# Two projection slots between the middle units of a four-unit cycle of an attention loop

## The chip, the cores and the metric

The kernel runs on one core of a Trainium2 chip. The metric is the device time of one execution in microseconds. A core has TensorE (PE in the profile; PEld are its weight loads), VectorE (DVE), ScalarE (ACT), GpSimd (POOL), SyncE (SP, which issues the DMAs here), a working memory SBUF and the accumulators PSUM, into which TensorE writes and from which VectorE and ScalarE read.

## The reference

One block of 2048 tokens of width 512, in float32. Two branches are mixed by a gate per token:

```python
g = sigmoid((x * gate_w).sum(-1, keepdims=True))
out = g * attention(x) + (1 - g) * glu(x)

# attention: 32 heads of 16, causal, window of 256 keys
qkv = x @ wqkv                                # 512 -> 3 * 512
scores = einsum("bhqd,bhkd->bhqk", q, k) * 16 ** -0.5
mask = (i - j >= 0) & (i - j < 256)
p = softmax(where(mask, scores, -1e9))
a = einsum("bhqk,bhkd->bhqd", p, v) @ wo

# gated linear unit, inner width 1376
b = (sigmoid(x @ w_gate) * (x @ w_up)) @ w_down
```

## The kernel before, in words

To keep float32 accuracy on a faster matmul type, most operands are split into a high part (a ScalarE cast) and a low part (a VectorE subtraction, raw minus high), and a product is made of three: high by high, high by low, low by high.

The program has three stages. First x and the weights are split, the values and the first query and key projections are made. Then comes the attention loop over 128 *units*: 8 groups of 4 heads, each with 16 blocks of 128 queries. Last, from 558 us on, come the down projection of the gated linear unit and the output projection. The change is in the loop.

A unit u has four *heads* h = 0 to 3, and each head emits, in the order of the code:

- s(u,h), `s_part`: the scores of one query block against up to three key blocks, one matmul of 64 contraction rows and up to 384 columns into a PSUM tile `s`. There are two such buffers. VectorE then adds the mask and takes the row maximum in one pass (L331, here *the reduction*; a short accumulator read follows). s(u,h) can't begin until the reduction of two heads before has left its buffer.
- st(u-9, h^1), `st_part`: nine units later, when the row maxima have come back by way of DRAM into spare contraction rows, the scores are computed again, transposed, into a PSUM tile `st` of three buffers; ScalarE takes the exponential (L380).
- one entry of a list of pending VectorE operations (`behind`) and one of pending ScalarE operations (`acts`).
- `run_slots(n)`: n *slots*. This is *gap* (u mod 4, h).

A slot is one step of the projections: work that does not depend on the attention of the unit. It holds two matmuls of 512 columns: one on contraction rows 0 to 63 for one group, one on rows 64 to 127 for a group that began 19 steps earlier (`SHIFT`). TensorE runs the two halves of its rows side by side; s and st of a head also take one half each. A group is one projected tile (`pj`, queries and keys; `gu`, gate and up) and takes 12 steps in each half; every 12 slots one group ends. At its end ScalarE copies it out of PSUM (L522 for `gu`, L270 for `pj`); three PSUM buffers (`misc`) are shared by the groups. A `pj` is then cast (L280, `sh`) and its low half subtracted (L284, `sl`), each one head later, through `acts` and `behind`. `gu` weights are split the same way (L506, L507), once per four groups, and the weights of a `pj` group of heads once per 16 units (L155, L157).

Every four units a *burst* multiplies the exponentials with the values (L428, `pvs` and `pvst`, in one `s` and one `st` buffer). It stands ahead of head 0 of units with u mod 4 = 2. ScalarE copies one half of it out (L442) and VectorE adds the other (L445). Behind the burst two slots run at once, and the gaps (2,0) and (2,1) have one slot less (`head`).

So a cycle of four units has had these slots, heads 0 to 3: u mod 4 = 0: 3, 3, 3, 3; 1: 3, 3, 3, 0; burst and 2; 2: 2, 2, 3, 3; 3: 3, 3, 3, 0. They are 42. At gap (1,3) the burst follows; at gap (3,3), between units 4k+3 and 4k+4, s(u,3) is followed by s(u+1,0) with nothing between but st. At the end of a unit 4k+3 three small VectorE operations (L343, L344, L347) are put into `behind` for the heads that follow.

The order is written out by hand: each engine runs its instructions in the order in which the code emits them, and semaphores hold them where an operand or a buffer is not ready.

Of the kernel before, what the change touches and what calls it, by code (L numbers as in the profile page):

```python
# [20 lines left out]
HG = 4  # L21
# [23 lines left out]
LAG = 9  # L45
# [3 lines left out]
HOLD = 2  # L49
GAP = 3  # L50
SHIFT = 19
WD_LATE = {0: 9, 2: 10}
WD_SPLIT = {0: 7, 1: 8, 3: 9, 5: 10}
AHEAD = 5
# [3 lines left out]
def gated_mix_kernel(  # L58
# [49 lines left out]
    NU = NG * NB  # L108
# [3 lines left out]
    def load_d(f):  # L112
        tag = "draw" if f in (6, 7) else "wqraw"
        raw_d[f] = cpool.tile([P, D], F32, tag=tag, name=f"wdraw{f}", bufs=2)
        nc.sync.dma_start(raw_d[f][0:FCH[f]], wd[f * P:f * P + FCH[f], :])
# [13 lines left out]
    with ExitStack() as actx:  # L129
# [14 lines left out]
        def load_wqk(g):  # L144
            raw = cpool.tile([P, ND, P], F32, tag="wqraw", name=f"wqraw{g}", bufs=2)
            nc.sync.dma_start(raw, wqk[g])
            return raw
# [138 lines left out]
        def stack_build(t):  # L286
            sh, sl = (v.bitcast(F32) for v in stg.pop(t))
            rt = ring[t % RING].bitcast(F32)
            st = rt.rearrange("(a r) j f -> r a j f", r=4)
            dmas = [fill_rows(t % RING, 0, 0)]  # L290
            for low in range(2):
                for j in range(4):
                    for r in range(3):
                        if low == (r == (1 if j < 2 else 2)):
                            dmas.append((st[r + 1, :, j], (sl if low else sh)[32 * j:32 * j + 32]))
            return dmas

        def run_dmas(dmas):
            for dst, src in dmas:
                nc.sync.dma_start(dst, src)  # L300
# [55 lines left out]
        def max_load(s):  # L356
            st = ring[s // 2 % RING].bitcast(F32).rearrange("(a r) j f -> r a j f", r=QB)
            o = s % 2 * CH
            nc.sync.dma_start(
                st[0, :, 0:2, o:o + CH], max_d[s].rearrange("(p s) l b t -> (s l) p (b t)", p=2),  # L360
            )
# [37 lines left out]
        def v_load(g):  # L399
            nc.sync.dma_start(  # L400
                vg[g % 2][:, 0:NB * GW].rearrange("p (b w) -> p b w", w=GW),
                v_d[:, :, g * GW:(g + 1) * GW].rearrange("b p w -> p b w"),
            )
# [90 lines left out]
        def load_gu(f, w):  # L494
            raw_gu[f, w] = cpool.tile([P, D], F32, tag="draw", name=f"guraw{f}_{w}", bufs=2)
            src = wgu[f, w] if FCH[f] == P else wgu_tail[w, :, :, 0:width(f, w)]
            nc.sync.dma_start(gu_half(raw_gu[f, w], width(f, w)), src)
# [63 lines left out]
        def turns():  # L561
            k3 = 3 * ND
            groups = []
            for t in range(n_rest * k3 + SHIFT):
                if t % k3 == 0 and len(groups) < n_rest:
                    groups.append((work or rest).pop(0))
                for half, v in enumerate((t, t - SHIFT)):
                    if 0 <= v < n_rest * k3:
                        groups[v // k3][0](v % k3, half)
                if t >= SHIFT and (t - SHIFT) % k3 == k3 - 1:  # L570
                    _, after, post = groups[(t - SHIFT) // k3]
                    post()
# [8 lines left out]
        def wo_load(t):  # L581
            raw = cpool.tile([P, CH2], F32, tag="hb", name=f"woraw{t}", bufs=4).rearrange("p (d n) -> p d n", d=2)
            nc.sync.dma_start(raw, wo_v[:, 2 * t:2 * t + 2])
            wo_raw.extend(raw[:, d] for d in range(2))

        def wo_split(d):
            nc.scalar.copy(wo_h[d], wo_raw[d])
            behind.append(lambda: nc.vector.tensor_tensor(
                wo_l[d], wo_raw[d], wo_h[d].bitcast(F32), op=ALU.subtract))

        def flush(acts):
            while acts:
                acts.pop(0)()
# [36 lines left out]
        def run_slots(n):  # L630
            for _ in range(n):
                next(slots, None)
# [22 lines left out]
        for u in range(N):  # L655
            if u == LAG + 2:
                vctx.close()
                ppool = actx.enter_context(tc.tile_pool(name="ppool", bufs=1))
                for k in range(2):
                    vg.append(ppool.tile([P, NB * GW + 16], F32, name=f"vg{k}"))  # L660
                    nc.gpsimd.memset(vg[k][:, NB * GW:], 0.0)
                hvs += [
                    v.rearrange("p (w t) -> p w t", t=CH)
                    for v in [vg[0][:, 0:2 * CH]] + [region[:, o:o + 2 * CH] for o in HVO]
                ]
            if u == LAG + 3 or u % NB == 0 and 0 < u < NU:
                v_load(u // NB)
            if u == 4:
                load_gu(0, 0)
                load_gu(0, 1)  # L670
            if (u % 8 == 1 and u > 16 or u == LAG + 1) and u // 8 + 1 < NP:
                sdma = stack_build(u // 8 + 1)
            if u % 16 == 8 and u // 16 + 2 < NG:
                raw_q = load_wqk(u // 16 + 2)
            if u % 4 == 1 and 1 < u <= NU + 1:
                max_load(u // 4 - 1)
            run_dmas(later)
            later.clear()
            run_dmas(sdma[:SD])
            del sdma[:SD]  # L680
            if u in (WO, WO + 2):
                wo_load((u - WO) // 2)
            if u == N - 4:
                acts.extend(lambda d=d: wo_split(d) for d in range(ND))
            if WD <= u < WD + 18 and (u - WD) % 2 == 0:
                load_d((u - WD) // 2)
            s4 = {U_LAST: NSTEP - 2, U_LAST + 1: NSTEP - 1}.get(u)
            if u % 4 == 3 and u > 11 and (u + 2) // 4 + 4 < NSTEP - 2:
                s4 = (u + 2) // 4 + 4
            if s4 is not None:  # L690
                work.append(proj_group(s4))
            if u >= NU + PVLAG - HOLD and rest:
                hold_group(*rest.pop(0))
            for hh in range(HG):
                if hh == 0 and u % 2 == 0:
                    if u in bursts:
                        pv_burst(*bursts[u])
                if hh == 0:
                    head = min(2, bursts.get(u, (0, 0))[1] // 2)
                    run_slots(head)  # L700
                if u < NU:
                    s_part(u, hh)
                if 0 <= u - LAG < NU:
                    st_part(u - LAG, hh ^ 1 if u < NU else hh)
                if u < LAG:
                    flush(behind)
                    run_slots(GAP)
                    flush(acts)
                    flush(behind)
                else:  # L710
                    if behind:
                        behind.pop(0)()
                    if acts:
                        acts.pop(0)()
                if hh == 2 and u % 4 == 0 and 0 < u <= NU:
                    max_store(u // 4 - 1)
                if u >= LAG and (hh < HG - 1 or u % 2 == 0 or u >= NU):
                    run_slots(GAP - (hh < head))
            if u % 4 == 3 and u < NU:
                behind[0:0] = max_split(u // 4)  # L720
            if u // 16 + 2 < NG:
                if u % 16 == 13:
                    acts.append(lambda g=u // 16 + 2, r=raw_q: (
                        split_wqk(g, r, 0), behind.append(lambda: split_wqk(g, r, 1))))
            if 0 <= u - LAG < NU:
                mask_p(u - LAG)
            if WD + 2 <= u < WD + 16 and (u - WD) % 2 == 0:
                acts.append(lambda f=(u - WD) // 2 - 1: split_d(f, True))
            if SUMS <= u and (u - SUMS) % 4 == 0:
                sums_load((u - SUMS) // 4)  # L730
            if SUMS + 2 <= u and (u - SUMS) % 4 == 2:
                behind.append(lambda c=(u - SUMS) // 4: later.append(sums_invert(c)))
            if u >= HLOAD and (u - HLOAD) % 2 == 0:
                h_load((u - HLOAD) // 2)
            if u >= N - 2:
                flush(acts)
                flush(behind)
            if u >= N - 4:
                run_dmas(later)
                later.clear()  # L740
                if u < N - 1:
                    h_skew(u - N + 1)
# [43 lines left out]
        for n, (c, f) in enumerate(steps):  # L786
# [3 lines left out]
            h_skew(n)  # L790
            if n in WD_LATE:
                load_d(WD_LATE[n])
            if n in WD_SPLIT:
# [87 lines left out]
```

## Time and profile before

| | |
|---|---|
| median of 3 runs | 738.99 us (738.47 to 740.3) |
| profiled execution, own time | 738.34 us |
| its span (first to last instruction) | 736.6 us |
| granted TensorE clock | 1.00 throughout |

Busy time of the engines by stretch of the span, in us:

| stretch | PE | PEld | DVE | ACT |
|---|---|---|---|---|
| 50 to 80 | 29.50 | 27.31 | 22.88 | 10.43 |
| 80 to 505 (loop) | 424.98 | 347.20 | 289.98 | 285.68 |
| 505 to 560 | 55.00 | 45.38 | 24.11 | 39.32 |
| 560 to 736.6 | 172.89 | 139.99 | 106.10 | 77.27 |

How to read the lines: a group's line names the source line, engine, operation, the tiles out<-in, partitions and elements, the count, then busy time and mean ns of one, then the idle time of the engine just before it and what ended most of that. A waits line says who waited for whom: us in total, times, longest. A timeline line has start in us, duration in us, engine, source line, operation, tiles, count, and in brackets the idle time before it with its releaser. Matmuls are pipelined: the next one of a half starts while the last still drains, so the pace of TensorE is read from start to start, and its busy share is not a measure of its pace.

### The profile page before, as it was taken

The numbers are of one execution on the slowest core, as the hardware profiler recorded it, in microseconds if no ns is written. First come the engines' busy times: TensorE is split into PE (matmuls) and PEld (weight loads), VectorE is DVE, ScalarE is ACT, GpSimd is POOL, SyncE is SP. The second block draws the span as 40 slices with busy tenths as digits, with TensorE's granted clock in tenths as the row PEclk, the third lists the DMA queues.
The fourth block names the chain that finished last, engine by engine and source line by source line (L and its number), as shares of the span: only waits on it lengthen the run. The fifth ranks groups of instructions, "written<-read, shape, count | busy, mean of one in ns | idle before, by whom it ended". The sixth has DMA issues, their size and how long they took to land.

```text
span 736.6 us, 20433 instructions
## 1 busy us (share of the span) xinstructions
PE 730.0 (99%) x7772; PEld 599.0 (81%) x7772; DVE 463.2 (63%) x1425; ACT 434.2 (59%) x898; POOL 165.9 (23%) x256
## 2 busy tenths in 40 slices
PE   8999999999999999999999999999999999999997
PEld 7889888888878878888887878888887888888886
DVE  4437767766676666765677667666424777557471
ACT  5512776676676667666667666666676554535241
POOL 7000433233233223233223322332330000000000
PEclk9999999999999999999999999999999999999999
DMA  8473564455455355444545525653555868466441
GB/s 296 114 231 113 131 174 137 110 134 152 126 136 134 108 150 147 137 120 121 156 125 137 135 57 160 181 168 108 169 174 164 244 206 257 149 214 202 148 135 57
DMA packets 88753, 112.68 MB, mean 153 GB/s; under 512 B 36050, under 2 KB 45778, under 8 KB 88656
## 3 DMA queue, kind: packets, MB, share of 16 engines
q1 hardware_dynamic: 88656, 111.39, 51.7%
q8 instruction: 61, 1.00, 0.6%
q14 instruction: 36, 0.29, 0.1%
HBM read 49.72 MB, written 36.45 MB: 117 GB/s over the span
## 4 chain that ended last, share of the span: by engine, by line
PE 98%; DMA 1%; DVE 0%; ACT 0%; issue 0%; SPq 0%; DVEq 0%
PE gu L258 37%; PE pj L258 10%; PE pvs L428 8%; PE s L325 7%; PE pd L80 6%; PE pd L82 5%; PE pd L81 5%; PE st L375 5%; PE vps L240 3%; PE pa L80 2%; PE pa L82 2%; PE pa L81 2%; PE pvst L428 2%; PE vps L80 1%; PE vps L81 1%; PE vps L82 1%
## 5 line engine op out<-in xcount | busy, mean ns | idle before, releaser
L331 DVE CUSTOM_DVE_ANT_0 junk<-s,mask 128x384 f32<-128x384 f32 (+2 forms) x512 | 266.5, 530 | 153.8 <-PE st L375 89.4
L258 PE MATMUL gu<-xh,w 64*128 64x512 f32 (+2 forms) x1392 | 352.5, 394 | 0.0
L380 ACT ACTIVATE region<-st 128x384 f32<-128x384 f32 (+2 forms) x512 | 239.2, 475 | 101.4 <-PE st L375 54.1
L258 PE MATMUL gu<-xl,w 64*128 64x512 f32 (+2 forms) x696 | 243.8, 394 | 0.0
L258 PEld LDWEIGHTS gu<-xh,w 64*128 64x128 f32 (+2 forms) x1392 | 204.9, 182 | 16.0 <-issue 0.8
L385 POOL TENSOR_SCALAR_AFFINE_SELECT region<-region 128x512 f32<-128x512 f32 x128 | 84.6, 661 | 378.3 <-ACT region L380 336.4
L375 PE MATMUL st<-ring 64*128 64x384 f32 (+2 forms) x536 | 168.5, 326 | 0.0
L325 PE MATMUL s<-ring 64*128 64x384 f32 (+2 forms) x536 | 167.1, 326 | 0.5 <-DVE mx L331 0.5
L258 PEld LDWEIGHTS gu<-xl,w 64*128 64x128 f32 (+2 forms) x696 | 124.9, 183 | 10.0 <-issue 2.0
L325 PEld LDWEIGHTS s<-ring 64*128 64x128 f32 x536 | 98.1, 184 | 28.7 <-DVE mx L331 18.5
L375 PEld LDWEIGHTS st<-ring 64*128 64x128 f32 x536 | 97.5, 184 | 6.9 <-ACT region L380 0.2
L258 PE MATMUL pj<-xh,wqh 64*128 64x512 f32 (+1 forms) x240 | 94.5, 399 | 0.0
L258 PE MATMUL pj<-xl,wqh 64*128 64x512 f32 (+1 forms) x240 | 93.0, 393 | 0.0
L428 PE MATMUL pvs<-region,vg 64*32 64x320 f32 (+4 forms) x1440 | 74.5, 346 | 0.0
L258 PE MATMUL pj<-xh,wql 64*128 64x512 f32 (+1 forms) x240 | 74.3, 396 | 0.0
L428 PE MATMUL pvst<-region,vg 64*32 64x320 f32 (+4 forms) x1440 | 73.1, 341 | 0.0
L390 POOL TENSOR_SCALAR_AFFINE_SELECT region<-region 128x512 f32<-128x512 f32 x112 | 72.0, 643 | 0.0
L428 PEld LDWEIGHTS pvs<-region,vg 64*32 64x32 f32 x1440 | 49.0, 106 | 26.8 <-issue 9.8
L80 PE MATMUL pd<-ring,hb 128*128 128x512 f32 (+1 forms) x176 | 69.4, 394 | 0.0
L82 PE MATMUL pd<-ring,hb 128*128 128x512 f32 (+1 forms) x176 | 68.9, 392 | 0.0
L81 PE MATMUL pd<-ring,hb 128*128 128x512 f32 (+1 forms) x176 | 68.6, 390 | 0.0
L76 ACT CAST hb<-region 128x512 fp32r<-128x512 f32 (+1 forms) x37 | 23.0, 622 | 51.5 <-DVE region L614 36.4
(83 smaller groups left out, 1040.1 us busy)
## 6 DMA issues: line engine op xcount, KB each, us to landing
gu_scratch<-sp SPq DMA_DIRECT2D x80, 256.0 KB
region<-gu_scratch SPq DMA_DIRECT2D x68, 256.0 KB
ring<-sh SPq DMA_DIRECT2D x128, 128.0 KB
ring<-sl SPq DMA_DIRECT2D x64, 128.0 KB
guraw<-in_wgu_dram SPq DMA_DIRECT2D x20, 256.0 KB
v_scratch<-region SPq DMA_DIRECT2D x16, 272.0 KB
vg<-v_scratch SPq DMA_DIRECT2D x8, 544.0 KB
region<-in_xT_dram SPq DMA_DIRECT2D x16, 256.0 KB
```

Of the source, the lines that this page charges most:

```text
L76: nc.scalar.copy(hi, src)
L80: mm(ps, lh, rh, start=first, stop=False)
L81: mm(ps, lh, rl, start=False, stop=False)
L82: mm(ps, ll, rh, start=False, stop=last)
L258: mm(pt[0:fw], (wl if w == 2 else wh)[r, d], (xl if w == 1 else xh)[r, d, c * CH:(c + 1) * CH], start=k == 0 and half != 1, stop=k == 3 * ...
L325: mm(pt[:, (k - k0) * P:(e - k0) * P], lhsT, blk(g, k, hh, 1, e - k), start=k == k0, stop=e == i + 1, skip_group_check=True,)
L331: nc.vector.tensor_tensor_reduce(junk[:, 0:n], pt[:, 0:n], mask[:, 3 * P - n:], scale=1.0, scalar=NEG, op0=ALU.add, op1=ALU.max, accum_out ...
L375: mm(pt[:, (q - j) * P:(e - j) * P], lhsT, blk(g, q, hh, 0, e - q), start=q == j, stop=e == last, skip_group_check=True,)
L380: nc.scalar.activation(pts[u][:, hh, 0:n], pt[:, 0:n], AF.Exp, scale=SCALE)
L385: nc.gpsimd.affine_select(p[:, :, 0:P], p[:, :, 0:P], pattern=[[0, HG], [1, P]], compare_op=ALU.is_ge, fill=0.0, base=0, channel_multiplie ...
L390: nc.gpsimd.affine_select(p[:, :, 2 * P:], p[:, :, 2 * P:], pattern=[[0, HG], [-1, P]], compare_op=ALU.is_gt, fill=0.0, base=0, channel_mu ...
L428: mm(acc[half][32 * hh:32 * hh + 32, q0:q1], vg[g % 2][r, c:c + 32], pts[g * NB + j][r, hh, q0 + o:q1 + o], start=m == 0, stop=m == len(or ...
```

## The change

The number of slots of a gap comes from a table by u mod 4 and head, from unit 12 on; before that, and behind the last unit of scores, nothing changes. Gap (3,3) gets 2 slots where it had none; gaps (1,1) and (3,1) have 2 where they had 3. The sum of a cycle stays 42. (1,3), ahead of the burst, stays 0.

```diff
+GAPS = ((3, 3, 3, 3), (3, 2, 3, 0), (3, 3, 3, 3), (3, 2, 3, 2))
...
-                if u >= LAG and (hh < HG - 1 or u % 2 == 0 or u >= NU):
-                    run_slots(GAP - (hh < head))
+                if u >= LAG:
+                    run_slots((GAP if u >= NU else GAPS[u % 4][hh] if u > LAG + 2 else GAP * (u % 2 == 0 or hh < HG - 1)) - (hh < head))
```

No instruction is added or removed; some change places. The new table is one line, so the lines of the changed kernel behind it have numbers higher by one. Three places follow, with the names in full: s67_3 is s of unit 67, head 3; the last number of a name only counts tiles.

TensorE, from s(67,3) to the first slots of unit 68 (gap (3,3)), before:

```order
L325 MATMUL s67_3_5135<-ring_63 128x384
L375 MATMUL st58_2_5139<-ring_63 128x384
L325 MATMUL s68_0_5150<-ring_63 128x384
L375 MATMUL st59_1_5154<-ring_63 128x384
L258 MATMUL pj21_5115<-xh_70,wqh5_4733 128x512
```

and now:

```order
L326 MATMUL s67_3_5131<-ring_63 128x384
L376 MATMUL st58_2_5135<-ring_63 128x384
L259 MATMUL pj21_5115<-xh_70,wqh5_4731 128x512
L259 MATMUL gu4_2_0_4925<-xh_70,w0_72 128x512
L259 MATMUL pj21_5115<-xl_71,wqh5_4731 128x512
L259 MATMUL gu4_2_0_4925<-xh_70,w0_72 128x512
L326 MATMUL s68_0_5150<-ring_63 128x384
```

Two slots, four matmuls, now stand between the two s.

TensorE, gap (1,1) of unit 69, before:

```order
L325 MATMUL s69_1_5232<-ring_63 128x384
L375 MATMUL st60_0_5236<-ring_63 128x384
L258 MATMUL gu4_0_1_5192<-xh_70,w0_72 128x512
L258 MATMUL pj21_5115<-xh_70,wqh5_4733 128x512
L258 MATMUL gu4_0_1_5192<-xh_70,w0_72 128x512
L258 MATMUL pj21_5115<-xl_71,wqh5_4733 128x512
L258 MATMUL gu4_0_1_5192<-xh_70,w0_72 128x512
L258 MATMUL pj21_5115<-xh_70,wqh5_4733 128x512
L325 MATMUL s69_2_5246<-ring_63 128x384
```

and now:

```order
L326 MATMUL s69_1_5232<-ring_63 128x384
L376 MATMUL st60_0_5236<-ring_63 128x384
L259 MATMUL gu4_0_1_5192<-xh_70,w0_72 128x512
L259 MATMUL pj21_5115<-xh_70,wqh5_4731 128x512
L259 MATMUL gu4_0_1_5192<-xh_70,w0_72 128x512
L259 MATMUL pj21_5115<-xl_71,wqh5_4731 128x512
L326 MATMUL s69_2_5244<-ring_63 128x384
```

The third slot of the gap has gone to the gap behind it, and everything up to gap (3,1) stands one slot later against s and st, from there to gap (3,3) two.

VectorE, unit 70, where a projection ends one slot later against the heads and its low half (sl) follows, before:

```order
L331 ISA junk70_2_5355,mx17_5149<-s70_2_5353,mask_155 128x384
L331 ISA mx17_5149 128x1
L284 TENSOR_TENSOR sl20_5099<-pr21_5339,sh20_5098 128x512
L331 ISA junk70_3_5369,mx17_5149<-s70_3_5367,mask_155 128x384
L331 ISA mx17_5149 128x1
```

and now:

```order
L332 ISA junk70_2_5352,mx17_5149<-s70_2_5350,mask_155 128x384
L332 ISA mx17_5149 128x1
L332 ISA junk70_3_5366,mx17_5149<-s70_3_5364,mask_155 128x384
L332 ISA mx17_5149 128x1
L285 TENSOR_TENSOR sl20_5097<-pr21_5346,sh20_5096 128x512
```

The subtraction stands behind the reduction of head 3 instead of that of head 2. So it is with every odd projection from 9 to 29 (units 22, 30, ... 102); the even ones, 8 to 28 (units 19, 27, ... 99), keep their place between the reductions of heads 1 and 2 of unit 4k+3.

## The prediction

> **What bounds the kernel now.** I read the busy shares and the groups of the page first, then the waits, then the timeline around the place that is changed.
>
> ```profile
> PE 730.0 (99%) x7772; PEld 599.0 (81%) x7772; DVE 463.2 (63%) x1425; ACT 434.2 (59%) x898; POOL 165.9 (23%) x256
> ...
> L331 DVE CUSTOM_DVE_ANT_0 junk<-s,mask 128x384 f32<-128x384 f32 (+2 forms) x512 | 266.5, 530 | 153.8 <-PE st L375 89.4
> L325 PE MATMUL s<-ring 64*128 64x384 f32 (+2 forms) x536 | 167.1, 326 | 0.5 <-DVE mx L331 0.5
> L325 PEld LDWEIGHTS s<-ring 64*128 64x128 f32 x536 | 98.1, 184 | 28.7 <-DVE mx L331 18.5
> ...
> PEld s L325 <- DVE mx L331: 18.5, 71, 0.9
> PEld st L375 <- ACT region L380: 0.2, 1, 0.2
> ```
>
> TensorE sets the end. Its matmul rows hardly show a wait (0.5 us ahead of s), because a matmul that is still draining counts as busy. The weight loads do show it: 71 of the loads of s stood 18.5 us for VectorE, those of st 0.2 us for ScalarE. So the one wait of the loop is that of s for one of its two PSUM buffers, which the reduction of two heads before (L331) has to leave.
>
> The page "Perfetto Trace Analysis" of the Trainium skill, section "Identifying the Most-Contended Engine", says that matmul busy time is no good measure of the distance to the roofline, and that the busy share of the weight loads serves better. The two L325 rows agree: by the first this change could win at most 0.5 us, by the second up to some 18.5 us stand ahead of the s loads.
>
> How much of such a wait costs time is read at unit 67 to 68, the old direct succession from gap (3,3).
>
> ```profile
> 294.10 0.34 PE L325 MATMUL s<-ring 64*128 64x384 f32 x1
> 294.27 0.39 PE L258 MATMUL pj<-xl,wqh 64*128 64x512 f32 x1
> 294.51 0.39 PE L258 MATMUL pj<-xh,wqh 64*128 64x512 f32 x1
> ...
> 294.95 0.33 PE L325 MATMUL s<-ring 64*128 64x384 f32 x1
> 295.29 0.44 PE L325 MATMUL s<-ring 64*128 64x384 f32 x1
> 295.57 0.39 PE L258 MATMUL pj<-xh,wqh 64*128 64x512 f32 x1
> ...
> 294.73 0.18 PEld L325 LDWEIGHTS s<-ring 64*128 64x128 f32 x1
> 295.29 0.18 PEld L325 LDWEIGHTS s<-ring 64*128 64x128 f32 x1 [0.36 <-DVE mx L331]
> ...
> 294.07 0.69 DVE L284 TENSOR_TENSOR sl<-pr,sh 128x512 fp32r<-128x512 f32 x1
> 294.67 0.55 DVE L331 CUSTOM_DVE_ANT_0 junk<-s,mask 128x384 f32<-128x384 f32 x1
> ```
>
> An undisturbed s takes 0.17 us (294.10 to 294.27) and a slot 0.24 (294.27 to 294.51; over many slots 0.233). Here s(68,0) follows s(67,3) after 0.34 us, 0.17 late: its buffer is that of s(67,2), whose reduction began only at 294.67, behind the low-half subtraction sl, and is left 0.62 us later. Then a second price: normally the load runs 0.22 us ahead of its matmul (294.73 to 294.95), under the slot before. This one starts with its matmul, which takes 0.44 instead of 0.33 us, and the next slot comes 0.28 us behind it (295.57) instead of 0.17. So **0.17 of wait and 0.11 of exposed load, 0.28 us in all**.
>
> **The change, part by part.** Every cycle of four units keeps 42 slots, every matmul and copy stays, so nothing is added to the sum of TensorE's work. Two slots now stand between s(u,3) and s(u+1,0) where the middle units meet, and gaps (1,1) and (3,1) have two instead of three. The profiled execution's own time is 738.34 us.
>
> *Part A: cycles with a subtraction in gap (3,1).* In the order of the program these are the units 19, 27, ... 99 (the even projections 8 to 28, eleven) and 123 (a weight split in its place): twelve. The VectorE order there is unchanged, so the reduction of s(67,2) still starts at 294.67 (s itself, a slot earlier, would allow 294.25), and the buffer is free at 295.29. s(67,3) moves from 294.95 to 294.72, and s(68,0) is due 0.17 + 2 x 0.233 = 0.64 later, at 295.36: 0.07 us behind the release instead of 0.17 before it. Its load is then 0.07 early where it wants 0.22. The row that is nearest:
>
> ```profile
> 291.38 0.18 PEld L325 LDWEIGHTS s<-ring 64*128 64x128 f32 x1 [0.20 <-DVE mx L331]
> 291.47 0.35 PE L325 MATMUL s<-ring 64*128 64x384 f32 x1
> 291.66 0.40 PE L258 MATMUL pj<-xh,wql 64*128 64x512 f32 x1
> ```
>
> A load only 0.09 ahead costs 0.02 us (0.19 to the next slot against 0.17). So 0.26 us are won of 0.28, 12 x 0.26 = 3.1 us. Bounds: 12 x 0.28 = 3.4, and 12 x 0.17 = 2.0 if the load stays exposed.
>
> *Part B: the other cycles*, 17 from unit 15 to 127, without a subtraction there.
>
> ```profile
> 188.67 0.33 PE L325 MATMUL s<-ring 64*128 64x384 f32 x1
> 188.87 0.44 PE L325 MATMUL s<-ring 64*128 64x384 f32 x1
> 189.15 0.39 PE L258 MATMUL pj<-xh,wqh 64*128 64x512 f32 x1
> ...
> 188.87 0.18 PEld L325 LDWEIGHTS s<-ring 64*128 64x128 f32 x1 [0.17 <-DVE mx L331]
> ...
> 188.24 0.56 DVE L331 CUSTOM_DVE_ANT_0 junk<-s,mask 128x384 f32<-128x384 f32 x1 [0.32 <-PE s L325]
> ```
>
> VectorE was idle ahead of this reduction, so it is the bare succession that exposes the load: 0.28 to the next slot, 0.11 lost. Where tiles at the start of a head group are narrow it is less; 280.13 to 280.25 for a 128-column s (0.06 by width) loses 0.06:
>
> ```profile
> 280.13 0.28 PE L325 MATMUL s<-ring 64*128 64x128 f32 x1
> 280.25 0.44 PE L258 MATMUL pj<-xh,wqh 64*128 64x512 f32 x1
> ```
>
> With two slots between, s(40,0) is due at 188.67 + 0.64 = 189.31 and its buffer free at 188.24 + 0.62 = 188.86, 0.45 us ahead: the load is hidden. 16 cycles at 0.09, between the two rows, give 1.4 us (bounds 16 x 0.06 = 1.0 and 16 x 0.11 = 1.8; I leave one cycle out for the edges of the loop).
>
> *Part C: units 30, 46, 62, 78, 94*, where a weight split, the burst's addition and the subtraction sl crowd VectorE.
>
> ```profile
> 276.90 0.68 DVE L284 TENSOR_TENSOR sl<-pr,sh 128x512 fp32r<-128x512 f32 x1
> 277.50 0.55 DVE L331 CUSTOM_DVE_ANT_0 junk<-s,mask 128x384 f32<-128x384 f32 x1
> 277.98 0.55 DVE L331 CUSTOM_DVE_ANT_0 junk<-s,mask 128x384 f32<-128x384 f32 x1
> ...
> 277.03 0.44 PE L325 MATMUL s<-ring 64*128 64x384 f32 x1
> 278.11 0.44 PE L325 MATMUL s<-ring 64*128 64x384 f32 x1
> 278.39 0.39 PE L258 MATMUL gu<-xh,w 64*128 64x512 f32 x2
> ```
>
> s(63,1) is due at 277.03 + 0.28 + 3 x 0.233 = 278.01, comes at 278.11 with its load exposed: 0.10 + 0.11 = 0.21 us lost. The group's end moves a slot back past s(62,1), and with it copy, cast and sl go one head back. Then the reduction of s(62,3) runs at 276.90 and leaves s(63,1) free at 277.52; sl runs at 277.38 and the next reduction at 277.98, as now, so s(63,2) is free at 278.60 and due, after the shorter gap, at 278.65. That load is late and costs 0.04. Against it, the projection's raw copy stands behind one more exponential, and the group that takes its PSUM buffer may start some 0.1 late. I take 0.10 of the 0.21: 5 x 0.10 = 0.5 us (bounds 0 and 1.0).
>
> *The two shortened gaps*, 29 each. Two-slot gaps stand behind the burst already:
>
> ```profile
> 273.96 0.33 PE L325 MATMUL s<-ring 64*128 64x384 f32 x1
> 274.60 0.33 PE L325 MATMUL s<-ring 64*128 64x384 f32 x1
> 275.23 0.33 PE L325 MATMUL s<-ring 64*128 64x384 f32 x1
> ...
> 300.12 0.56 DVE L331 CUSTOM_DVE_ANT_0 junk<-s,mask 128x384 f32<-128x384 f32 x1 [0.30 <-PE s L325]
> ```
>
> They run at 0.64 us, 0.17 + 2 x 0.233, with no loss. A reduction takes 0.48 us when the next one waits (277.50 to 277.98), so it keeps up at 0.64, and at gap (1,1) VectorE even sat idle 0.30 us. Outside A and C I price this at 0; its upper bound is an exposed load at each, 58 x 0.11 = 6.4 us.
>
> **Sum:** 3.1 + 1.4 + 0.5 = 5.0 us. 738.34 - 5.0 = 733.3 us for a profiled execution; the median of the runs lies 0.65 above that execution, so **734.0 us**.
>
> **Rivals.** *The load stays exposed.* If the releases of A and C come a tenth later, the waits go but the loads still start with their matmuls: 2.0 + 1.4 + 0 = 3.4 us, 735.6. For it: the margin in A is only 0.07. Against: sl and the reduction keep their places.
>
> *The load can't be hidden at all*, so that only the wait of A is won: 738.99 - 2.0 = 737.0. Against it stands the load of 294.73, under a matmul of its own rows. The Trainium skill's page "TensorE: Matmul & The Clock Gate", section "The mechanism" of its part on packing, says that a weight load overlaps running matmuls only when its row group differs; by that rule every succession pays its load and this rival is the result. The trace disagrees: the load at 294.73 begins while slot matmuls run in both halves (the one of 294.51 until 294.90), and its s took 0.33.
>
> *VectorE decides at the shortened gaps* (slower): each of the 58 would have its load exposed and stand 0.06 us, 58 x 0.17 = 9.9 us lost against 5.0 won, 743.9. It decides as soon as the buffer's release, 0.62 behind a reduction's start, falls after the next s but one; the idle 0.30 speaks against it at (1,1), at (3,1) only A and C come near.
>
> *The change moves the wait and wins nothing*: s(u,2) or st stand instead. 739.0.
>
> **How the numbers follow.** My forecast has 0.62, the exposed load 0.18, the load that is never hidden 0.07, the moved wait 0.07, VectorE at the shortened gaps 0.06. All upper bounds together win 3.4 + 1.8 + 1.0 = 6.2 us, 732.8. The range 732.6 to 737.2 takes in the first three. A measurement tells about 0.3% (2.2 us) from no change: faster, under 736.8, has 0.62 + 0.18 = 0.80; within it the next two, 0.14; slower 0.06.
>
> **What would show it.** The waiting of the s loads for VectorE should fall by about 12 x (0.36 - 0.15) + 16 x 0.17 = 5.2 us, from 18.5 to near 13. s(68,0) should follow s(67,3) after 0.64 us and take near 0.33; st should still not wait. If the s loads of units 4k+1 and 4k+3 at head 2 show waits of 0.3 us, the third rival holds; if the waits shrink and the s matmuls still take 0.44 us, the first. If PE's waits vanish and the time stays, I have misread what a wait costs.

## The result, and the profile after

The changed kernel takes 732.62 us (median of 6 runs, 731.94 to 733.17) against 738.73 us (6 runs, 737.74 to 742.51) for the kernel before. The ratio is 0.9907, 95% interval 0.9891 to 0.9924: 0.93% or 6.9 us faster, between 5.6 and 8.1. By the difference of the medians it is 6.1 us. The forecast was faster by 5.0 us, 734.0 us; the direction and the mechanism were right and the size was too small: 732.62 lies at the very edge of the range, and the ratio's 6.9 us beyond the 6.2 us of all upper bounds together.

The page and the waits of the changed kernel (lines are one higher than before):

```profile
PE 723.8 (99%) x7772; PEld 601.0 (82%) x7772; DVE 461.4 (63%) x1425; ACT 437.7 (60%) x898; POOL 167.3 (23%) x256
...
L326 PE MATMUL s<-ring 64*128 64x384 f32 (+2 forms) x536 | 167.1, 321 | 0.5 <-DVE mx L332 0.5
L326 PEld LDWEIGHTS s<-ring 64*128 64x128 f32 x536 | 98.4, 184 | 21.6 <-DVE mx L332 12.7
...
PEld s L326 <- DVE mx L332: 12.7, 54, 0.9
```

The loads of s wait 12.7 us in 54 places instead of 18.5 us in 71. The matmul row of s still shows 0.5 us of idle time, as before, and TensorE is still 99% busy: by that row alone nothing has happened. This is the case of which the Trainium skill's page "Perfetto Trace Analysis", section "Identifying the Most-Contended Engine", warns. The busy share of the weight loads, which that section would have read instead, moved only from 81 to 82%; what tells the change here is the waiting time ahead of the loads.

The timeline at unit 67 to 68, the place that the prediction worked out (TensorE, its loads, VectorE):

```profile
291.08 0.33 PE L326 MATMUL s<-ring 64*128 64x384 f32 x1
291.94 0.33 PE L326 MATMUL s<-ring 64*128 64x384 f32 x1
292.60 0.35 PE L326 MATMUL s<-ring 64*128 64x384 f32 x1
292.79 0.39 PE L259 MATMUL pj<-xh,wqh 64*128 64x512 f32 x1
...
292.50 0.18 PEld L326 LDWEIGHTS s<-ring 64*128 64x128 f32 x1 [0.18 <-DVE mx L332]
...
291.28 0.69 DVE L285 TENSOR_TENSOR sl<-pr,sh 128x512 fp32r<-128x512 f32 x1
291.89 0.55 DVE L332 CUSTOM_DVE_ANT_0 junk<-s,mask 128x384 f32<-128x384 f32 x1
```

s(68,0) follows s(67,3) after 0.66 us with two slots between, where it took 0.34 with none. Its reduction still starts 0.61 behind the start of sl, the buffer is free at 292.50, 0.61 later, and the load runs 0.10 us ahead of its matmul; the next slot comes after 0.19 us instead of 0.28.

In a bare succession of before, s(40,0) took 0.44 us and 0.28 to the next slot of its half. Now:

```profile
187.15 0.33 PE L326 MATMUL s<-ring 64*128 64x384 f32 x1
187.78 0.33 PE L326 MATMUL s<-ring 64*128 64x384 f32 x1
187.96 0.39 PE L259 MATMUL pj<-xh,wqh 64*128 64x512 f32 x1
...
187.56 0.18 PEld L326 LDWEIGHTS s<-ring 64*128 64x128 f32 x1
```

The load runs 0.22 us ahead, without a wait, and the slot follows after 0.18.

To see where the time went, the loop is measured from the start of s(14,0) to that of s(126,0), with the same work between in both kernels (first the two rows of before, then of the change):

```profile
91.13 0.33 PE L325 MATMUL s<-ring 64*128 64x384 f32 x1
517.33 0.33 PE L325 MATMUL s<-ring 64*128 64x384 f32 x1
```

```profile
91.28 0.33 PE L326 MATMUL s<-ring 64*128 64x384 f32 x1
511.35 0.33 PE L326 MATMUL s<-ring 64*128 64x384 f32 x1
```

426.20 us became 420.07: 6.13 us less. Cut into the cycles from s(4k+2,0) to s(4k+6,0), and added up by the prediction's kinds (A twelve, B eleven, C five; the twelfth B, of unit 127, lies outside), the change of each kernel told of below against the kernel before, in us:

| kernel | loop | A | B | C |
|---|---|---|---|---|
| the change | -6.13 | -2.75 | -1.93 | -1.45 |
| one slot at (3,3), from (3,1) | -1.92 | +0.01 | -1.50 | -0.44 |
| short gaps, none at (3,3) | -0.34 | +0.08 | -0.40 | -0.01 |
| even sl held back | -2.33 | -2.13 | -0.18 | -0.03 |
| two slots at (3,3), both from (3,1) | -1.82 | +0.05 | -1.63 | -0.24 |
| odd sl one head later | -0.65 | +0.06 | +0.02 | -0.73 |
| third slot at (3,1) | -5.73 | -2.99 | -1.54 | -1.21 |
| more room, short gaps in a row | -7.18 | -3.47 | -1.44 | -2.27 |
| more room, short gaps apart | -8.20 | -3.92 | -1.99 | -2.28 |
| more room, short gaps early | -8.45 | -4.07 | -1.99 | -2.40 |

Each is one profiled execution. Where a kernel leaves a kind of cycle as it was, the table still shows up to 0.08 us. The spans are steadier than the times: s(14,0) itself starts between 89.1 and 91.4 us in these executions. The tables leave out at most three slots ahead of it (0.7 us), and the kernels that leave out none there spread from 89.6 to 91.4 all the same; that goes into every time.

### The profile page after: what moved, and what is told of

Read it like the earlier page. It is cut to its first block, busy times and chain, and to the rows that moved or that the text cites. A ratio compares the mean times of both kernels' runs of the same rounds, so it can differ in the third digit from the quotient of the medians.

```text
span 731.0 us, 20428 instructions
## 1 busy us (share of the span) xinstructions
PE 723.8 (99%) x7772; PEld 601.0 (82%) x7772; DVE 461.4 (63%) x1425; ACT 437.7 (60%) x898; POOL 167.3 (23%) x256
## 4 chain that ended last, share of the span: by engine, by line
PE 97%; DMA 2%; DVE 1%; ACT 0%; SPq 0%; issue 0%; DVEq 0%
PE gu L259 37%; PE pj L259 11%; PE pvs L429 8%; PE s L326 6%; PE st L376 5%; PE pd L81 5%; PE pd L83 5%; PE pd L82 5%; PE vps L241 3%; PE pa L81 2%; PE pa L83 2%; PE pa L82 2%; PE pvst L429 2%; PE vps L81 1%; PE vps L82 1%; PE vps L83 1%
## 5 line engine op out<-in xcount | busy, mean ns | idle before, releaser
L259 PE MATMUL gu<-xh,w 64*128 64x512 f32 (+3 forms) x1392 | 357.5, 394 | 0.0
L381 ACT ACTIVATE region<-st 128x384 f32<-128x384 f32 (+2 forms) x512 | 242.5, 476 | 92.3 <-PE st L376 44.1
L259 PE MATMUL gu<-xl,w 64*128 64x512 f32 (+2 forms) x696 | 246.8, 393 | 0.0
L259 PEld LDWEIGHTS gu<-xh,w 64*128 64x128 f32 (+3 forms) x1392 | 203.3, 183 | 19.0 <-issue 2.4
L259 PEld LDWEIGHTS gu<-xl,w 64*128 64x128 f32 (+2 forms) x696 | 123.0, 183 | 5.7 <-issue 0.4
L326 PEld LDWEIGHTS s<-ring 64*128 64x128 f32 x536 | 98.4, 184 | 21.6 <-DVE mx L332 12.7
L259 PE MATMUL pj<-xl,wqh 64*128 64x512 f32 (+1 forms) x240 | 95.3, 402 | 0.0
```

Source lines behind the costliest of these rows:

```text
L259: mm(pt[0:fw], (wl if w == 2 else wh)[r, d], (xl if w == 1 else xh)[r, d, c * CH:(c + 1) * CH], start=k == 0 and half != 1, stop=k == 3 * ...
L326: mm(pt[:, (k - k0) * P:(e - k0) * P], lhsT, blk(g, k, hh, 1, e - k), start=k == k0, stop=e == i + 1, skip_group_check=True,)
L381: nc.scalar.activation(pts[u][:, hh, 0:n], pt[:, 0:n], AF.Exp, scale=SCALE)
```

## The experiments

The slot tables are given against that of the change, `((3,3,3,3), (3,2,3,0), (3,3,3,3), (3,2,3,2))`.

**One slot at (3,3).**

```diff
-GAPS = ((3, 3, 3, 3), (3, 2, 3, 0), (3, 3, 3, 3), (3, 2, 3, 2))
+GAPS = ((3, 3, 3, 3), (3, 3, 3, 0), (3, 3, 3, 3), (3, 2, 3, 1))
```

> One slot instead of two at gap (3,3), taken from gap (3,1); gap (1,1) keeps three. Theory (two prices of the direct succession, a wait and an exposed weight load): with one slot s(40,0) is due 0.40 us behind s(39,3) and its buffer is free 0.2 us ahead, so the load is hidden in the cycles without a late subtraction and what B and C win of it in the changed kernel (1.9 us over 11 B cycles, 0.5 to 0.9 over C) is won here too; in the twelve A cycles s(68,0) is due at 295.12 and its buffer free at 295.29, so wait and exposed load stay and nothing is won. Sum about 2.5 us less than the kernel before (736.2). Rival 1, only the wait of A costs time: 0. Rival 2, any separation of the two s will do: about 6 us less, as the change.

735.82 us; ratio to before 0.9965 (0.9951 to 0.9979), 2.6 us faster. The table shows it by kinds: A won nothing, B 1.50 of the 1.93 us that the change won, C 0.44 of 1.45. Unit 68 and unit 40, the rows of s with its load and the next slot:

```profile
292.38 0.33 PE L326 MATMUL s<-ring 64*128 64x384 f32 x1
292.96 0.44 PE L326 MATMUL s<-ring 64*128 64x384 f32 x1
293.24 0.39 PE L259 MATMUL pj<-xh,wqh 64*128 64x512 f32 x1
292.95 0.18 PEld L326 LDWEIGHTS s<-ring 64*128 64x128 f32 x1 [0.36 <-DVE mx L332]
...
186.71 0.43 PE L259 MATMUL gu<-xh,w 64*128 64x512 f32 x2
186.94 0.33 PE L326 MATMUL s<-ring 64*128 64x384 f32 x1
186.72 0.18 PEld L326 LDWEIGHTS s<-ring 64*128 64x128 f32 x1
```

With one slot s(68,0) still stands for its buffer, 0.58 us behind s(67,3) where 0.40 would do, and still takes 0.44. s(40,0) has its load 0.22 ahead. The two prices come apart: one slot saves the exposed load, and only the second one, brought from gap (1,1), saves the wait of A. One sentence of the Trainium skill's page "TensorE: Matmul & The Clock Gate", section "The mechanism", lets a load overlap running matmuls only when its row group differs; an earlier sentence of that section also allows it for a load into a background weight buffer. The trace speaks against the first taken alone: the load of s(40,0) starts at 186.72, right behind the start of slot matmuls in both halves (186.71), and s takes 0.33.

**The shortened gaps alone.**

```diff
+GAPS = ((3, 3, 3, 3), (3, 2, 4, 0), (3, 3, 3, 3), (3, 2, 4, 0))
```

> The two gaps (1,1) and (3,1) shortened to two slots, as in the change, but the slots go to the gaps just behind them, (1,2) and (3,2); gap (3,3) stays without slots. Theory: the shortened gaps cost nothing and win nothing, and the succession at (3,3) is as before: within 0.7 us of the kernel before. Rival, part of the gain comes from the shortened gaps themselves: 2 us less or more. The slower rival of the prediction, VectorE decides at the shortened gaps: up to 6 us more.

738.55 us; ratio 0.9997 (0.9983 to 1.0012). The loop is 0.34 us shorter, which lies in the B cycles of units 23, 71 and 119. The loads of s wait as much as before:

```profile
PEld s L326 <- DVE mx L332: 19.1, 71, 0.9
```

But in the B cycles they wait one head later. Units 39 and 40, from s(39,3) to s(40,1):

```profile
188.80 0.33 PE L326 MATMUL s<-ring 64*128 64x384 f32 x1
188.98 0.34 PE L326 MATMUL s<-ring 64*128 64x384 f32 x1
189.79 0.44 PE L326 MATMUL s<-ring 64*128 64x384 f32 x1
...
188.87 0.18 PEld L326 LDWEIGHTS s<-ring 64*128 64x128 f32 x1
189.79 0.18 PEld L326 LDWEIGHTS s<-ring 64*128 64x128 f32 x1 [0.21 <-DVE mx L332]
```

s(40,0) still follows s(39,3) with no slot between, yet its load leads by 0.11 us and it takes 0.34; now s(40,1) has the exposed load. s(40,0) takes the buffer of s(39,2), and s(40,1) that of s(39,3). So it is not the bare succession as such that exposes a load, as the prediction had it, but too few slots in two neighbouring gaps: three in (3,2) and (3,3) before, three in (3,3) and (0,0) here. With four in such a pair, and no subtraction between, the load leads: by 0.11 us here and by 0.22 with one slot at (3,3).

The run therefore moves a loss instead of leaving it alone, and by itself it doesn't prove the two-slot gaps free. The changed kernel does: from unit 14 to 125 every load of s(4k+1,2) leads by 0.2 us or more, and so does every load of s(4k+3,2) but those of the five C cycles, which lead by 0.07 to 0.11. The slower rival of the prediction falls.

**The subtraction taken away from A.** In the kernel before, with its own slots, sl of the even projections waits until the next unit:

```diff
-                    if behind:
+                    if behind and not (behind[0] in held and 11 < u < NU and u % 4 == 3):
                         behind.pop(0)()
```

(`held` lists the functions that subtract; they are appended to `behind` as before.)

> The kernel before with its slots as they were; only the subtraction sl of the even projections is held out of units 4k+3 and runs at gap (0,3) of the next unit. That takes the late reduction of A away without a slot between the two s. Theory: in eleven cycles the wait of 0.17 us goes, 1.9 us, while the load of s(u+1,0) stays exposed (s(68,0) takes 0.44 us), so the kernel is about 1.9 us faster (736.8). Rival, the exposed load is only the shadow of the wait and goes with it: 3.1 us faster. Rival, the wait isn't that of the subtraction: 0.

736.31 us; ratio 0.996 (0.9946 to 0.9975), 3.0 us faster; in the loop 2.3, nearly all in A, 0.19 us in each of the eleven cycles. The wait was that of sl. At unit 68:

```profile
292.27 0.33 PE L325 MATMUL s<-ring 64*128 64x384 f32 x1
292.48 0.39 PE L325 MATMUL s<-ring 64*128 64x384 f32 x1
292.71 0.39 PE L258 MATMUL pj<-xh,wqh 64*128 64x512 f32 x1
...
292.43 0.18 PEld L325 LDWEIGHTS s<-ring 64*128 64x128 f32 x1 [0.17 <-DVE mx L331]
```

The load of s(68,0) is only partly exposed here: it leads by 0.05, s takes 0.39 and the slot follows after 0.23. So the result, by the loop, lies between the theory's 1.9 and the rival's 3.1.

**Two slots at (3,3), both from (3,1).**

```diff
+GAPS = ((3, 3, 3, 3), (3, 3, 3, 0), (3, 3, 3, 3), (3, 1, 3, 2))
```

> Two slots at gap (3,3) as in the change, but both taken from gap (3,1), which is left with one; gap (1,1) keeps three. Theory: in A what counts is the slots between the subtraction's reduction and s(u+1,0), and these are six as before the change (1+3+2), so s(68,0) is due at 295.13 while its buffer is free at 295.29: A wins nothing, B and C win their loads, about 2.5 us less than before (736.2), unless the one-slot gap, 0.40 us against 0.48 us of a reduction, costs 0.11 in some cycles. Rival, two slots between the two s are what counts: about 6 us less, as the change.

736.43 us; ratio 0.9971 (0.9957 to 0.9985), 2.1 us faster, and not the change's 6.9. Two slots between the two s, as in the change, and yet:

```profile
293.87 0.33 PE L326 MATMUL s<-ring 64*128 64x384 f32 x1
294.67 0.44 PE L326 MATMUL s<-ring 64*128 64x384 f32 x1
294.67 0.18 PEld L326 LDWEIGHTS s<-ring 64*128 64x128 f32 x1 [0.41 <-DVE mx L332]
```

s(68,0) stands 0.80 us behind s(67,3), where 0.64 was due. What decides in A is the number of slots between the subtraction and s(u+1,0), and that grew in the change only because one came from gap (1,1).

**The odd subtraction one head later.** Again the kernel before, with its own slots:

```diff
+                    if behind and not (behind[0] in held and 11 < u < NU and u % 4 == 2 and hh == 2):
```

> The kernel before with its slots as they were; only the subtraction sl of the odd projections is held back by one head, from gap (2,2) to (2,3), as it comes to stand in the changed kernel. Theory: this is what part C won beyond the load at (3,3): the C cycles (units 31, 47, 63, 79, 95) are 0.2 us shorter each, by their own spans in the trace, A and B as before; 1.0 us in all, at the edge of what the times tell. Rival, C's gain came from the shortened gap (3,1) or from the slots at (3,3): C cycles as before.

738.01 us; ratio 0.999 (0.9979 to 1.0001): by the times not told from no change. By the spans the C cycles are 0.15 us shorter each, A and B as before. s(63,0), s(63,1) and the VectorE row between:

```profile
276.85 0.44 PE L325 MATMUL s<-ring 64*128 64x384 f32 x1
277.90 0.33 PE L325 MATMUL s<-ring 64*128 64x384 f32 x1
...
277.19 0.69 DVE L284 TENSOR_TENSOR sl<-pr,sh 128x512 fp32r<-128x512 f32 x1
```

s(63,1) now takes 0.33 where it took 0.44. Moving sl makes 0.15 and the load at (3,3) 0.09 (one slot: 0.44 over five), together 0.23 of C's 0.29 in the change; where the rest comes from the runs don't show.

**A third slot again at (3,1).**

```diff
+GAPS = ((3, 3, 3, 2), (3, 2, 3, 0), (3, 3, 3, 3), (3, 3, 3, 2))
```

> The changed kernel, with a third slot again at gap (3,1), taken from gap (0,3) (now two). So s(u+1,0) of an A cycle comes one slot later against the reduction that holds it. Theory: its buffer is then free 0.3 us ahead, the load is wholly hidden and A wins the rest of the 0.28 us, 0.05 more per cycle than the change (0.6 us over twelve); B and C as in the change; the shortened (0,3) costs nothing. So 0.6 us under the change (about 732). Rival, what A still loses isn't the late load: no difference from the change. Rival, gap (0,3) with two slots brings VectorE to its pace: 29 x 0.11 = 3 us slower than the change.

732.93 us; ratio to before 0.992 (0.9903 to 0.9937); by the times as the change. A won 0.02 us more per cycle than in the change, 0.249 instead of 0.229, and not 0.05: with the load wholly hidden an A cycle wins 0.25 us, so 0.28 had been too much. One C cycle (unit 95) came out 0.3 us longer here than in the change. In the trace the load of the st behind s(95,0) stands 0.18 us there for the DMA of the row maxima (393.02), and s(95,1) comes 0.27 us later behind s(95,0) than in the kernel before; in the change that load waits for no DMA.

**More room ahead of s(u,0) of units 4k+3.** One slot more at (2,1) (the table's 4 less one behind the burst).

```diff
+GAPS = ((3, 3, 3, 2), (2, 2, 3, 0), (3, 4, 3, 3), (3, 3, 3, 2))
```

> As the kernel with the third slot at (3,1), and one slot more behind the burst at gap (2,1), taken from gap (1,0): three gaps in a row, (0,3), (1,0), (1,1), have two slots. The loads of s(u,0) of units 15, 19, 31, 47, 51, 63, 79, 83, 95, 115, 127 still wait 0.32 to 0.38 us for VectorE in the changed kernel, where a weight split crowds unit 4k+2. Theory: one more slot ahead of s(u,0) hides that, about 0.06 + 0.11 = 0.17 us in eleven cycles, 1.9 us, together with A's rest 2.4 us under the change (about 730). Rival, three short gaps in a row are too much for VectorE (0.64 us each against 0.48 of a reduction, with small operations between): the loads at (1,0) to (1,2) wait instead, 0 or slower than the change.

731.97 us; ratio to before 0.9908 (0.9892 to 0.9925), by the times as the change; the loop is 1.05 us shorter than with the change, where 2.4 were expected.

```profile
PEld s L326 <- DVE mx L332: 4.2, 15, 0.9
```

The waits went as expected, and with them a late load that I had not priced: that of s(4k+2,3), only 0.07 to 0.16 us ahead in every unit 4k+2 of the loop, before and in the change. But five cycles lost 0.15 to 0.22 us against the next kernel below, those with a weight split at gap (1,0) or (1,1), among the three short gaps. Unit 45:

```profile
206.04 0.33 PE L326 MATMUL s<-ring 64*128 64x384 f32 x1
206.83 0.44 PE L326 MATMUL s<-ring 64*128 64x384 f32 x1
206.83 0.18 PEld L326 LDWEIGHTS s<-ring 64*128 64x128 f32 x1 [0.40 <-DVE mx L332]
...
205.62 0.69 DVE L508 TENSOR_TENSOR w<-guraw,w 128x512 fp32r<-128x512 f32 x1
206.22 0.55 DVE L332 CUSTOM_DVE_ANT_0 junk<-s,mask 128x384 f32<-128x384 f32 x1
```

s(45,2) comes 0.79 us behind s(45,1), 0.15 late, and its load is exposed: s(45,2) takes the buffer of s(45,0), whose reduction starts 0.60 behind the start of w, the subtraction of the split; the buffer comes free 0.61 later, at 206.83.

**The short gaps apart.**

```diff
+GAPS = ((3, 2, 3, 2), (3, 2, 3, 0), (3, 4, 3, 3), (3, 3, 3, 2))
```

> The kernel with more room at (2,1) and (3,1), but its short gaps apart: (0,1), (0,3) and (1,1) have two slots, (1,0) has three again. In the kernel with (0,3), (1,0) and (1,1) short in a row the loads of s(u,0) waited no longer, yet s(45,2) came 0.26 us late behind a weight split at (1,0), and the bursts of units 57 and 89 0.2 us. Theory: VectorE keeps up with one short gap and not with three in a row when a 0.69 us split falls among them; with the short gaps apart these seven losses of about 0.25 us go, 1.7 us, so the loop is about 2.5 us shorter than in the changed kernel (about 730.2). Rival, the splits at (1,0) cost the same behind any two short gaps: as the kernel with three in a row (732).

730.43 us against 738.49 of before beside it; ratio 0.988 (0.986 to 0.99), 1.2% faster. The losses behind the weight splits went, the loop is 2.1 us shorter than with the change (2.5 expected). The cycle of unit 103 won only 0.05 us against before, where the change had won 0.35: the load of s(104,2) waits for its buffer again. What is left of the waits:

```profile
PEld s L326 <- DVE mx L332: 3.3, 14, 0.9
```

**The short gaps early.**

```diff
+GAPS = ((2, 3, 2, 3), (3, 2, 3, 0), (3, 4, 3, 3), (3, 3, 3, 2))
```

> As the kernel with the short gaps apart, but the short gaps are (0,0), (0,2) and (1,1); (0,0) lies where VectorE has the first of the three small operations of the row maxima (0.36 us) between reductions. Theory: 0.64 us still hold a reduction of 0.48 but not one with 0.36 more and a subtraction in A cycles ahead of it, so s(u,2) of units 4k+4 waits in some cycles: up to 12 x 0.1 us slower than the kernel with (0,1), (0,3), (1,1) short. Rival: no difference.

730.40 us; ratio 0.9889 (0.9871 to 0.9908). No loss at (0,0): the rival held, and the small operation of the row maxima still fits. By the loop these two tables beat the change, by 2.1 and 2.3 us, in one execution each; the intervals of their ratios overlap that of the change, and each other.

Not tried: a fourth slot at gap (2,3) or (2,2).

## Where the prediction was right, and the term that it mis-sized

*What bounds the kernel.* Right: the only wait in the loop that mattered was that of s for its buffer, and it shows in the loads, not in the matmuls. The forecast of the waits, 18.5 to near 13 us, met 12.7.

*Two prices of a succession, a wait and an exposed load.* Right, and shown apart by the run with one slot and by the run with sl held back. They are not quite two: the load is hidden by degrees (below). And the second is not the price of the bare succession itself: with a fourth slot at (3,2), s(40,0) followed bare and had its load nearly hidden.

*Part A*, forecast 3.1 us, measured 2.75. The release and the due time came as worked out (0.10 us ahead instead of 0.07). The 0.28 was 0.03 too high, as the third slot at (3,1) showed with 0.25 won; it had been read from one place with two-figure rows, where 0.34 and 0.17 leave 0.17 of a wait and the spans say less.

*Part B*, the mis-sized term. I priced a bare succession at 0.09 us, between two rows, for 16 cycles, five of which were C's, so 1.0 for the eleven B cycles of the table; they won 1.93. Two rows, read in the half of TensorE that runs s, stood for eleven cycles that differ. Of the 0.94 us that B won beyond the forecast, 0.46 lies in three cycles (units 23, 71, 119), at whose next units the ring of key and query blocks wraps and s comes in two pieces: they won 0.24 to 0.26. Unit 24, from s(24,0) on, before and then in the change:

```profile
127.72 0.38 PE L325 MATMUL s<-ring 64*128 64x256 f32 x1
127.83 0.32 PE L375 MATMUL st<-ring 64*128 64x128 f32 x1
127.99 0.44 PE L258 MATMUL gu<-xl,w 64*128 64x512 f32 x1
128.01 0.45 PE L258 MATMUL pj<-xh,wqh 64*128 64x512 f32 x1
```

```profile
127.67 0.27 PE L326 MATMUL s<-ring 64*128 64x256 f32 x1
127.68 0.22 PE L376 MATMUL st<-ring 64*128 64x128 f32 x1
127.74 0.44 PE L259 MATMUL gu<-xl,w 64*128 64x512 f32 x1
127.85 0.44 PE L259 MATMUL pj<-xh,wqh 64*128 64x512 f32 x1
```

The half that runs s goes on with pj 0.29 us behind the start of s(24,0) before and 0.18 now, the 0.11 of the prediction. The half that runs st goes on with gu after 0.27 before and 0.07 now: it had lost 0.20. That these 0.20 make up the gain of these cycles is not shown; the shortened gaps alone, where the exposed load stands at s(24,1), won 0.12 to 0.14 in them, and one slot 0.16 to 0.28. Another 0.26 lies in unit 103, which won 0.35: it is no bare succession, projection 30 has its sl at gap (3,3), late for s(104,2); with that sl held back the cycle won 0.23. I had sorted the cycles by the even projections and missed that one. The other seven won 0.12 on average (0.06 to 0.21), in all 0.22 us more than priced. In these, too, the price left something out: in the kernel before, the load of s(u+1,1) led by 0.06 to 0.13 us only, and now by 0.23.

*Part C*, forecast 0.5 beside its load, about 0.9 to 1.0 with it; measured 1.45. Of the two costs that I set against the gain, the late load at s(63,2) came about as priced: it led by 0.07 us (276.09 to 276.16), s took 0.37, and s(63,3) came 0.04 us later behind it than before. The late raw copy, the rest of what I took off, doesn't show: in units 30, 46, 62, 78 and 94 the steps from s to s are those of before within 0.02 us. What moved sl is shown by the run that moves only sl.

*The shortened gaps at no cost.* Right outside C, as the leads of their loads in the changed kernel show; in C they cost the 0.04 us above. The kernel with three of them in a row shows where it ends.

*The rivals.* The load that stays exposed would have won 3.4 us and A would have shown 0.44 us matmuls: nine of the twelve cycles show 0.34 to 0.38, so it falls there. In three (units 20, 52 and 84, behind a weight split that holds up the unit ahead) the load does start with its matmul, s takes 0.43 us and the next slot follows after 0.28. These cycles won 0.21 to 0.24 us like the others all the same, and a third slot at (3,1) added 0.03 us to each: s(u+1,0) follows s(u,3) after 0.57 to 0.58 us there, instead of 0.62 to 0.67 in the nine, which makes up for most of the late slot. The load that can't be hidden falls by s(40,0). VectorE at the shortened gaps and the moved wait fall by the times. The range was too narrow on the side of the gain, because its low end was the sum of the upper bounds, and that of B, 0.11 us a cycle, was taken from one row that is not of the kinds that won most.

## What to carry to other kernels

Where matmuls are pipelined, look for waits in the weight loads, and for matmuls that take longer than their like: a load that starts with its matmul costs as much as a short wait. Filling work is best put not where an engine seems idle but between the producer that frees a buffer late and its next user; two slots in the right gap won 1.82 of the loop's 6.13 us when they came from just ahead of it. Where two buffers take turns, count the work in two neighbouring gaps together, since the buffer is that of two users before. And before a price from one cycle is multiplied, sort all cycles by what stands in them.

## What the runs showed of the hardware that was not expected

The load of 0.18 us hides by degrees, and a lead of 0.05 us is enough to halve its price. Time from s to the next slot, by how far its load led: 0.22 us ahead 0.17 to 0.18 (187.56 and 187.78), 0.10 ahead 0.19 (292.50), 0.05 ahead 0.23 (292.43), none 0.28 (292.95).
